# Hash attention with a feed-forward block: k and q read once and transposed on TensorE for the first batch, weights staged in pieces, feed-forward issued over the whole next batch

## The chip, the cores and the metric

One core of a Trainium2 chip. The metric is the device time of one execution in microseconds (us). "Profile" means the record of one profiled execution, "span" its length (about 2 us less than the time on the clock of the runs). The program runs on one core, so there is no second die to compare; runs more than 1.5% above the fastest of the same kernel are set aside as slow.

Engines: PE is TensorE, PEld its weight loads, DVE VectorE, ACT ScalarE, POOL GpSimd, SP the engine that issues most DMAs (SPq is its queue of instructions).

## The reference, cut to what matters

```python
# q, k, v: (4 batches, 8 heads, 768 tokens, 64); proj: (64, 6)
q_bucket = sum((q @ proj > 0) * 2**arange(6));  k_bucket likewise
scores = where(q_bucket == k_bucket, q @ k.T / 8, -1e9)
attn   = softmax(scores) @ v                    # per head
x      = attn as (4, 768, 512)                  # heads side by side
xn     = (x - mean) / sqrt(var + 1e-6) * g_ln
out    = x + max(xn @ w_ch1, 0) @ w_ch2         # 512 -> 2048 -> 512
```

The last line needs all heads of a batch, so a batch has two stages: attention, then feed-forward.

## The kernel before

The mask is folded into the score matmul: each row of q and k gets six extra columns (its hash bits as plus or minus one half, on the q side times a large number), so a score matmul contracts 64 + 6 = 70 rows. A "unit" is four heads; there are 8 units, two per batch. Attention is a chain of 192 steps (24 per unit). A step is one `scores` (two matmuls, one exp of 128x768 on ACT) and one `attend` of two steps earlier (six small matmuls). Preparation of the next unit, normalization, stores and feed-forward are put into the steps by a table, `at(step, function, ...)`, and each engine is given its share in that order.

Preparing a unit reads k and q twice, in two layouts: "hash" rows for the bits, "score" rows for the operand. The padded operand is then transposed by DMA:

```python
load_hash(...)                                   # hashnat: for the bits
load_rows(...)                                   # scorenat: for the operand
pad[:, :, 0:64] = cast(scorenat)                 # POOL
hashT = 32x32 transposes of hashnat              # DVE
hp    = projT.T @ hashT                          # PE, f32, four column groups side by side
pad[:, :, 64:70] = (transposed hp > 0) - 0.5     # DVE
opT   = DMA transpose of pad                     # SP queue
```

The feed-forward of a batch is a generator that yields after each of its 224 matmuls. This is the loop that drives it, cut (`...`):

```python
LAG, FF_DELAY, N_FF, BATCH, TAIL_MM = 2, 7, 224, 48, 45
# first[b] = b*48 + 1 + 48 + 7:  56, 104, 152, 200;   n_steps = 192
for b in range(B):
    z = b * BATCH + LAG - 1
    ...
    at(z + BATCH, rstd, b)                 # statistics, four Newton rounds: DVE
    at(z + BATCH, normalize, b, 0)         # DVE
    at(z + BATCH + 1, turn_x, b, 0)        # DMA transpose: xT
    at(z + BATCH + 1, normalize, b, 1)
    at(z + BATCH + 3, turn_x, b, 1)
while ...:
    scores(i); attend(i - LAG); run_step(i)
    if first[b] == i: ffq.append(feed_forward(b))
    if i < n_steps:
        target = 0.0
        for b in range(B):
            left = TAIL_MM if b == B - 2 else 0
            span = BATCH if b < B - 2 else n_steps - first[b]
            target += (N_FF - left) * min(max((i + 1 - first[b]) / span, 0.0), 1.0)
    else:
        target = done + 7
    while ffq and done < target:
        next(ffq[0]); done += 1
    i += 1
```

The f32 weights (8.4 MB) come in 1 MB pieces through two buffers (`hbuf`), from before step 0 to about step 43, and are cast by DVE.

The softmax here doesn't subtract the row's maximum and nothing guards it: scores larger than these inputs give would overflow.

Of the kernel before, what the change touches and what calls it, by code (L numbers as in the profile page):

```python
# [9 lines left out]

F32 = mybir.dt.float32
BF16 = mybir.dt.bfloat16
I32 = mybir.dt.int32
AOP = mybir.AluOpType
# [4 lines left out]
def kernel(  # L19
# [11 lines left out]
    nc = tc.nc  # L31
    P = 128

    B, H, S, D = q.shape
    NB = proj.shape[1]
    DM = moe_g_ln.shape[0]
    HID = moe_w_ch1.shape[1]
    assert DM == H * D and D == 64 and S == 768

    NS = S // P  # L40
    UH = 4
    NU = H // UH
    SL = UH * NS
    KB = D + NB
    VA = D + 1
    ND = DM // P
    NH = HID // P
    HALF = NS // 2
    QH = HALF * P

    scale = 1.0 / math.sqrt(D)
    BIG = 200.0
# [3 lines left out]
    consts = ctx.enter_context(tc.tile_pool(name="consts", bufs=1))  # L56
    prep = ctx.enter_context(tc.tile_pool(name="prep", bufs=1))
    work = ctx.enter_context(tc.tile_pool(name="work", bufs=1))
    ps_sc = ctx.enter_context(tc.tile_pool(name="ps_sc", bufs=2, space=bass.MemoryType.PSUM))
    ps_av = ctx.enter_context(tc.tile_pool(name="ps_av", bufs=2, space=bass.MemoryType.PSUM))  # L60
    ps_mm = ctx.enter_context(tc.tile_pool(name="ps_mm", bufs=2, space=bass.MemoryType.PSUM))
# [6 lines left out]
    proj_v = proj.rearrange("(j p) n -> p j n", p=32)  # L68
    for h in range(UH):
        nc.gpsimd.dma_start(  # L70
            out=projT[h * 32 : (h + 1) * 32, :, h * NB : (h + 1) * NB], in_=proj_v
        )
    bias_sb = consts.tile([P, 1], F32)
    nc.vector.memset(bias_sb, exp_bias)
    delta_m = consts.tile([P, P], BF16)
# [8 lines left out]
    g_sb = consts.tile([P, ND], F32)  # L84
# [8 lines left out]
    def at(i, fn, *args):  # L93
        todo.setdefault(i, deque()).append((fn, args))
# [7 lines left out]
    unit = {}  # L102
# [11 lines left out]
    def load_rows(ap, n, key, eng):  # L114
        b, u = divmod(n, NU)
        sn = prep.tile([P, UH, NS * D], F32, tag="scorenat", bufs=3, name="scorenat")
        eng.dma_start(
            out=sn,
            in_=ap[b, u * UH : (u + 1) * UH].rearrange("h (p s) d -> p h (s d)", s=NS),
        )  # L120
        loaded[(n, key, "rows")] = sn

    def pad_of(n, key):
        return pads[(2 * n + (key == "q")) % 3]

    def cast_rows(n, key):
        sn = loaded.pop((n, key, "rows"))
        nc.gpsimd.tensor_copy(  # L128
            pad_of(n, key)[:, :, 0:D], sn.rearrange("p h (s d) -> p (h s) d", d=D)
        )  # L130

    def hash_turn(n, key):
        hn = loaded.pop((n, key, "hash"))
        hT = prep.tile([P, 4, NS, 2, 32], F32, tag="hashT", bufs=1, name="hashT")
        for i in range(2):
            nc.vector.transpose(  # L136
                hT[:, 2 * i : 2 * i + 2].rearrange("p c s j t -> p (c s j t)"),
                hn[:, 2 * i : 2 * i + 2].rearrange("p c n -> p (c n)"),
            )
        half_done[(n, key)] = hT  # L140

    def hash_mm(n, key):
        hT = half_done.pop((n, key))
        hp = ps_mm.tile([P, 512], F32, tag="mm", name="hp")
        for j in range(2):
            for c in range(4):
                nc.tensor.matmul(  # L147
                    hp[c * 32 : (c + 1) * 32, 0 : NS * 32],
                    projT[:, j, :],
                    hT[:, c, :, j, :],  # L150
                    start=(j == 0), stop=(j == 1),
                )
        bits = prep.tile([P, NS, 32], F32, tag="bits", bufs=2, name="bits")
        nc.vector.transpose(bits.rearrange("p s n -> p (s n)"), hp[:, 0 : NS * 32])
        dst = pad_of(n, key).rearrange("p (h s) n -> p h s n", s=NS)[:, :, :, D:KB]
        src = bits[:, :, 0 : UH * NB].rearrange("p s (h n) -> p h s n", n=NB)
        nc.vector.tensor_scalar(
            dst, src, scalar1=0.0, scalar2=0.5, op0=AOP.is_gt, op1=AOP.subtract
        )
        if key == "q":  # L160
            nc.vector.tensor_scalar_mul(dst, dst, 4.0 * BIG)

    def turn(n, key, parts=1):
        tT = prep.tile([P, SL, P], BF16, tag="opT", bufs=4, name="opT")
        w = SL // parts
        for i in range(parts):
            nc.sync.dma_start_transpose(  # L167
                out=tT[:, i * w : (i + 1) * w, :],
                in_=pad_of(n, key)[:, i * w : (i + 1) * w, :].rearrange("p a n -> p (a n)"),
            )  # L170
        unit[(n, key)] = tT

    def value_cast(n):
# [18 lines left out]
    def plan_unit(n):  # L192

        z = (n - 1) * UNIT
        at(z + 0, cast_rows, n, "k")
        at(z + 0, hash_turn, n, "k")
        at(z + 3, hash_mm, n, "k")
        at(z + 5, turn, n, "k")
        at(z + 6, cast_rows, n, "q")
        at(z + 6, hash_turn, n, "q")  # L200
        at(z + 9, hash_mm, n, "q")
        at(z + 9, value_cast, n)
        at(z + 11, turn, n, "q")
        at(z + 15, value_sum, n)
        if n + 1 < B * NU:
            at(z + 3, load_hash, k, n + 1, "k", nc.sync)
            at(z + 3, load_rows, k, n + 1, "k", nc.sync)
            at(z + 9, load_hash, q, n + 1, "q", nc.sync)
            at(z + 9, load_rows, q, n + 1, "q", nc.sync)
            at(z + 15, load_rows, v, n + 1, "v", nc.sync)  # L210


    staged = {}

    def load_w1(o):
        st = work.tile([P, HID], F32, tag="hbuf", bufs=2, name="w1st")
        nc.sync.dma_start(out=st, in_=w1ap[:, o, :])
        staged[o] = st

    def fold_w1(o):  # L220
        nc.vector.tensor_scalar_mul(w1_sb[:, o, :], staged.pop(o), g_sb[:, o : o + 1])  # L221

    def load_w2(o):
        st = work.tile([P, 4, DM], F32, tag="hbuf", bufs=2, name="w2st")
        nc.sync.dma_start(out=st, in_=w2ap[:, o * 4 : (o + 1) * 4, :])
        staged[o] = st

    def cast_w2(o):
        nc.vector.tensor_copy(w2_sb[:, o * 4 : (o + 1) * 4, :], staged.pop(o))


    xs = {}
# [108 lines left out]
    def scores(i):  # L341
        b, u, h, t = steps[i]
        n = b * NU + u
        qT, kT = unit[(n, "q")], unit[(n, "k")]
        sc = ps_sc.tile([P, 2, 512], F32, tag="sc", name="sc")
        for f in range(2):
            nc.tensor.matmul(  # L347
                sc[:, f, 0:QH],
                kT[0:KB, h * NS + t, :],
                qT[0:KB, h * NS + f * HALF : h * NS + (f + 1) * HALF, :],  # L350
            )
        e = work.tile([P, 2, QH], BF16, tag="expb", bufs=4, name="expb")
        nc.scalar.activation(e, sc[:, :, 0:QH], AF.Exp, scale=scale, bias=bias_sb)  # L353
        exps[i] = e

# [31 lines left out]

    load_hash(k, 0, "k", nc.sync)
    load_hash(q, 0, "q", nc.scalar)
    load_rows(k, 0, "k", nc.sync)  # L390
    load_rows(q, 0, "q", nc.scalar)
    load_rows(v, 0, "v", nc.sync)
    for key in ("k", "q"):
        cast_rows(0, key)
        hash_turn(0, key)
        hash_mm(0, key)
        if key == "k":
            load_hash(k, 1, "k", nc.sync)
        turn(0, key, UH)
    value_cast(0)  # L400
    load_rows(k, 1, "k", nc.sync)
    load_hash(q, 1, "q", nc.sync)
    load_rows(q, 1, "q", nc.sync)
    value_sum(0)
    nc.sync.dma_start(out=g_sb, in_=moe_g_ln.rearrange("(o p) -> p o", p=P))
    load_w1(0)
    load_w1(1)
    load_rows(v, 1, "v", nc.sync)

    for n in range(1, B * NU):  # L410
        plan_unit(n)
    for o in range(4):
        at(8 + 5 * o, fold_w1, o)
        at(28 + 5 * o, cast_w2, o)
        if o < 2:
            at(8 + 5 * o, load_w1, o + 2)
            at(28 + 5 * o, load_w2, o + 2)
        else:
            at(8 + 5 * o, load_w2, o - 2)
    first = {}  # L420
    for b in range(B):
        z = b * BATCH + LAG - 1
# [15 lines left out]
    i = 0  # L438
    while i < n_steps + LAG + FF_DELAY + 1 or ffq or any(j >= i for j in todo):
        now[0] = i  # L440
        if i < n_steps:
            scores(i)
        if LAG <= i < n_steps + LAG:
            attend(i - LAG)
        run_step(i)
        for b in range(B):
            if first[b] == i:
                ffq.append(feed_forward(b))
        if i < n_steps:
            target = 0.0  # L450
            for b in range(B):
                left = TAIL_MM if b == B - 2 else 0
                span = BATCH if b < B - 2 else n_steps - first[b]
                target += (N_FF - left) * min(max((i + 1 - first[b]) / span, 0.0), 1.0)
# [3 lines that stand above are left out]
            try:  # L458
                next(ffq[0])
                done += 1  # L460
            except StopIteration:
                ffq.popleft()
        i += 1
# [30 lines left out]
```

## Time and profile before

| | before |
|---|---|
| time, median of 4 runs | 456.92 us (456.63 to 458.27) |
| span of the profile (of an execution of 459.3 us, slower than the four) | 457.5 us |
| PE busy / weight loads busy | 76% / 42% |
| DVE, ACT busy | 44%, 42% |

The first view is the page's table of 40 slices of 11.4 us. A digit is the busy share in tenths, PEclk the clock granted to PE, DMA the mean busy share of the 16 DMA engines. Ahead of the first clock record (30.2 us in this profile) the views print full clock, and that is no measurement: a hash took 2.35 us at 11.4 us, as long as at 75.4 us, where half clock is recorded, and 0.86 us at recorded full clock.

```profile
PE   0476247936499998856899998864999988449996
ACT  1065144844230329966112169952303199503020
PEclk9998555785799999996699999977999999759999
DMA  8999999995493017990961068965110130030101
```

Three regimes can be read. In slices 1 to 9 (to about 103 us) DMA is full while PE and ACT are half busy and PE's clock falls to half. From slice 11 on, ACT's row swings between 9 and 0: that is attention (ACT full, PE with gaps) alternating with feed-forward (PE full, ACT nearly idle). The last five slices are the tail: feed-forward of the last batch alone.

The alternation is plainer in the exps alone. This view gives the exp instruction (line 353) in six stretches: stretch and its length, busy time of ACT (number of exps that ran in it, whole or in part), granted clock, DMA share, GB/s. The DMA share can go above 1, since the whole time of a packet is counted in the stretch in which it starts.

```profile
60.00:72.00 12.00, 3.89 (x5) 0.50 1.12 268
144.00:156.00 12.00, 0.00 (x0) 1.00 0.12 44
168.00:180.00 12.00, 10.96 (x14) 1.00 0.63 154
240.00:252.00 12.00, 0.00 (x0) 1.00 0.12 45
276.00:288.00 12.00, 11.09 (x15) 1.00 0.86 197
336.00:348.00 12.00, 0.00 (x0) 1.00 0.13 49
```

Fifteen exps per 12 us is 0.79 us per step, ACT's limit; none at all runs during a feed-forward. At 60 us it is five.

Three waits of the first batch, the PE work of one step, and the wait before the last feed-forward, from the timeline: start, duration, engine, line, instruction, output and inputs, shapes, count, and in brackets how long the engine had been idle and what ended that.

```profile
54.07 0.38 PE L187 MATMUL vp<-vs,delta_m 128*128 128x260 bf16 x1 [9.66 <-POOL vs L181]
69.85 0.80 PE L347 MATMUL sc<-opT 70*128 70x384 bf16 x2 [7.64 <-DMA opT<-pad_85]
106.03 0.80 PE L347 MATMUL sc<-opT 70*128 70x384 bf16 x2 [10.13 <-DMA opT<-pad_87]
...
84.97 0.50 PE L347 MATMUL sc<-opT 70*128 70x384 bf16 x2
85.31 0.35 PE L364 MATMUL av<-vaug_92,expb 128*128 128x65 bf16 x6
85.49 0.49 PE L347 MATMUL sc<-opT 70*128 70x384 bf16 x2
...
406.98 1.44 PE L305 MATMUL h_4108<-xT,w_sb 128*128 128x384 bf16 x4 [11.65 <-DMA xT<-xn]
```

The first three are idle times of 8 to 10 us, at bottom waits for loads (vs is made from v, which had landed late) and for DMA transposes. Lines four to six show what a step costs PE when ACT does not hold it up: the next pair of score matmuls starts 0.52 us after the previous one. The Trainium skill, "TensorE: Matmul & The Clock Gate" (Step-by-step: what each phase is for), says that weight loads are pulled ahead of running matmuls; this trace agrees, since the six weight loads of `attend` take 0.38 us but matmuls and loads together take 0.52 us, less than the 0.32 us of the score matmuls plus 0.38 us.

### The profile page before, as it was taken

What the parts mean: (1) busy time and instruction counts of PE and PEld (TensorE: products, weight loads), DVE (VectorE), ACT (ScalarE), POOL (GpSimd) and SP (SyncE); (2) the same over time, 40 slices, a digit from 0 to 9 for tenths busy, and PEclk for the clock granted to TensorE, in tenths of its full rate; (3) what the DMA queues carried; (4) which work ended last, traced back from release to release, by engine and by line L of the source; (5) the groups of instructions that cost most, each with busy time, mean ns of one, the idle gap of its engine ahead of it and who ended that gap; (6) DMA issues with size and microseconds to landing.
All of it is one profiled execution on the core that took longest, in us unless ns stands there. A gap on an engine that the chain in (4) does not pass through costs nothing.

```text
span 457.5 us, 6762 instructions
## 1 busy us (share of the span) xinstructions
PE 345.7 (76%) x2688; PEld 190.4 (42%) x2696; DVE 202.7 (44%) x471; ACT 190.2 (42%) x257; POOL 71.0 (16%) x70
## 2 busy tenths in 40 slices
PE   0476247936499998856899998864999988449996
PEld 0143124524254545533445455532545455215452
DVE  1525125829832325949523227568323234642221
ACT  1065144844230329966112169952303199503020
POOL 5611513214011002314110004140000000000000
PEclk9998555785799999996699999977999999759999
DMA  8999999995493017990961068965110130030101
GB/s 200 282 202 352 193 277 356 249 291 128 111 243 129 1 69 177 223 225 6 249 182 47 23 123 210 225 114 110 28 71 0 70 71 1 1 69 1 69 1 69
DMA packets 91120, 62.32 MB, mean 136 GB/s; under 512 B 64976, under 2 KB 85456, under 8 KB 90576
## 3 DMA queue, kind: packets, MB, share of 16 engines
q1 hardware_dynamic: 89856, 60.31, 54.2%
q10 hardware_dynamic: 1104, 1.57, 1.3%
q8 instruction: 21, 0.34, 0.3%
q14 instruction: 11, 0.09, 0.1%
q0 software_dynamic: 128, 0.01, 0.0%
HBM read 39.85 MB, written 6.29 MB: 101 GB/s over the span
## 4 chain that ended last, share of the span: by engine, by line
PE 46%; DMA 21%; ACT 14%; DVE 9%; issue 4%; SPq 3%; POOL 1%; ACTq 0%; DVEq 0%
ACT expb L353 14%; DMA scorenat<-in_q_dram 4%; PE sc L347 3%; DMA scorenat<-in_k_dram 3%; DMA xT<-xn 3%; DMA opT<-pad_86 2%; DMA w1st<-in_moe_w_ch_dram 2%; DMA opT<-pad_85 2%; DMA opT<-pad_87 2%; PE hp L147 2%; SPq L167 2%; PE av L364 1%; DVE xn L275 1%; DMA hashnat<-in_q_dram 1%; DVE t L261 1%
## 5 line engine op out<-in xcount | busy, mean ns | idle before, releaser
L353 ACT ACTIVATE expb<-sc,bias_sb 128x768 bf16<-128x768 f32 x192 | 157.5, 921 | 106.4 <-PE sc L347 104.5
L347 PE MATMUL sc<-opT 70*128 70x384 bf16 x384 | 106.0, 361 | 45.4 <-DMA opT<-pad_85 11.4
L305 PEld LDWEIGHTS <-w_sb 128*128 128x128 bf16 x512 | 52.5, 103 | 78.2 <-issue 51.3
L364 PEld LDWEIGHTS <-expb 128*128 128x128 bf16 x1152 | 67.6, 105 | 33.4 <-issue 12.2
L347 PEld LDWEIGHTS <-opT 70*128 70x128 bf16 x384 | 35.2, 103 | 80.0 <-issue 79.2
L320 PEld LDWEIGHTS <-hbuf 128*128 128x128 bf16 x384 | 37.6, 98 | 45.7 <-issue 1.8
L376 DVE TENSOR_TENSOR nd<-av,vd 128x390 f32<-128x390 f32 x32 | 17.7, 554 | 45.0 <-PE av L364 45.0
L147 PE MATMUL hp<-hashT,projT 128*32 128x192 f32 x256 | 22.6, 436 | 17.9 <-DVE hashT L136 17.8
L136 DVE STREAM_TRANSPOSE hashT<-hashnat 128x768 f32<-128x768 f32 x32 | 29.2, 951 | 14.7 <-DMA hashnat<-in_k_dram 9.3
L364 PE MATMUL av<-vaug_91,expb 128*128 128x65 bf16 x432 | 28.1, 206 | 0.0
L364 PE MATMUL av<-vaug_92,expb 128*128 128x65 bf16 x432 | 27.5, 203 | 0.6 <-ACT expb L353 0.4
L382 DVE TENSOR_TENSOR x<-nd,rec 128x384 f32<-128x384 f32 x32 | 20.6, 643 | 1.1
L147 PEld LDWEIGHTS hp<-hashT,projT 128*32 128x32 f32 x256 | 8.9, 135 | 25.0 <-DVE hashT L136 21.5
L364 PE MATMUL av<-vaug_93,expb 128*128 128x65 bf16 x288 | 17.4, 198 | 0.0
L128 POOL CAST pad_85<-scorenat 128x1536 bf16<-128x1536 f32 x6 | 8.8, 1467 | 50.9 <-DMA scorenat<-in_k_dram 27.2
L238 DVE BATCH_NORM_STATS2 stats<-x 128x6 f32<-128x256 f32 (+1 forms) x48 | 16.1, 379 | 0.2
L179 POOL TENSOR_TENSOR scorenat<-scorenat 128x768 f32<-128x768 f32 x8 | 15.2, 1895 | 0.2
L128 POOL CAST pad_87<-scorenat 128x1536 bf16<-128x1536 f32 x5 | 7.3, 1467 | 50.4 <-DMA scorenat<-in_k_dram 30.4
L221 DVE TENSOR_SCALAR w_sb<-w1st,g_sb 128x2048 bf16<-128x2048 f32 x4 | 5.1, 1284 | 18.8 <-DMA w1st<-in_moe_w_ch_dram 18.8
L187 PE MATMUL vp<-vs,delta_m 128*128 128x260 bf16 x8 | 2.4, 299 | 13.3 <-POOL vs L181 13.3
L176 POOL CAST vaug_92<-scorenat 128x1536 bf16<-128x1536 f32 x3 | 4.4, 1472 | 51.3 <-DMA scorenat<-in_v_dram 51.3
L176 POOL CAST vaug_91<-scorenat 128x1536 bf16<-128x1536 f32 x3 | 4.7, 1582 | 45.6 <-DMA scorenat<-in_v_dram 45.5
(345 smaller groups left out, 383.5 us busy)
## 6 DMA issues: line engine op xcount, KB each, us to landing
hashnat<-in_k_dram SPq DMA_DIRECT2D x32, 192.0 KB, 4.9
scorenat<-in_k_dram SPq DMA_DIRECT2D x8, 768.0 KB, 7.4
scorenat<-in_v_dram SPq DMA_DIRECT2D x8, 768.0 KB, 5.6
out_dram<-x SPq DMA_DIRECT2D x24, 256.0 KB, 2.0
hashnat<-in_q_dram SPq DMA_DIRECT2D x28, 192.0 KB, 4.4
scorenat<-in_q_dram SPq DMA_DIRECT2D x7, 768.0 KB, 7.1
w1st<-in_moe_w_ch_dram SPq DMA_DIRECT2D x4, 1024.0 KB, 8.7
w2st<-in_moe_w_ch_dram SPq DMA_DIRECT2D x4, 1024.0 KB, 9.0
```

The costliest lines, as they stand in the source:

```text
L128: nc.gpsimd.tensor_copy(pad_of(n, key)[:, :, 0:D], sn.rearrange("p h (s d) -> p (h s) d", d=D))
L136: nc.vector.transpose(hT[:, 2 * i : 2 * i + 2].rearrange("p c s j t -> p (c s j t)"), hn[:, 2 * i : 2 * i + 2].rearrange("p c n -> p (c n)"),)
L147: nc.tensor.matmul(hp[c * 32 : (c + 1) * 32, 0 : NS * 32], projT[:, j, :], hT[:, c, :, j, :], start=(j == 0), stop=(j == 1),)
L179: nc.gpsimd.tensor_add(vn[:, :, 0:3, :], vn[:, :, 0:3, :], vn[:, :, 3:6, :])
L238: nc.vector.bn_stats(norm[b][:, s, part, :], xs[b][:, s, c0:c1])
L305: nc.tensor.matmul(hp[:, 0:QH], w1_sb[:, o, n * P : (n + 1) * P], xT[:, :, o, :], start=(o == 0), stop=(o == ND - 1),)
L320: nc.tensor.matmul(o2, hb[:, n, i * P : (i + 1) * P], w2_sb[:, n, :], start=(n == 0), stop=(n == NH - 1),)
L347: nc.tensor.matmul(sc[:, f, 0:QH], kT[0:KB, h * NS + t, :], qT[0:KB, h * NS + f * HALF : h * NS + (f + 1) * HALF, :],)
L353: nc.scalar.activation(e, sc[:, :, 0:QH], AF.Exp, scale=scale, bias=bias_sb)
L364: nc.tensor.matmul(av[:, s * VA : (s + 1) * VA], e[:, s // HALF, (s % HALF) * P : (s % HALF + 1) * P], va[:, h, t, :], start=(t == 0 and s ...
L376: nc.vector.tensor_add(nd, av[:, 0 : NS * VA].rearrange("p (s n) -> p s n", n=VA), vd[:, h : h + 1, :].to_broadcast([P, NS, VA]),)
L382: nc.vector.tensor_mul(xs[b][:, :, hd * D : (hd + 1) * D], nd[:, :, 0:D], rec.to_broadcast([P, NS, D]),)
```

## The change

Three things (smaller edits go with them: the loads of unit 2 are issued seven to ten steps later, `v` of the later units three steps earlier, and `expb` has three buffers instead of four):

1. Units 0 and 1 (the first batch) read k and q once, in hash layout. The operand comes from the same tile, and is transposed by PE (24 transposes per operand, copied out of PSUM by DVE or ACT) instead of by DMA. The hash bits then have to come out in another layout, for which the matmul uses a block-diagonal projection over the whole array and no longer four column groups side by side.
2. Weights are staged in 0.5 MB pieces: six in `hbuf` before step 0, six in the buffers of `x` that batch 1 and 2 will use, four in `hbuf` again.
3. The feed-forward target no longer counts the last batch. For it, `span` is 192 - 200 = -8, and `(i + 1 - 200) / -8` is at least 1 for every i below 192. So the target held 224 extra matmuls from the start, and every feed-forward was emitted whole in the step in which it began.

The diff, cut to its core:

```diff
+    projB = consts.tile([P, 2, P], F32)          # block-diagonal, one block per head
+    ident = consts.tile([P, P], BF16); make_identity(nc, ident)
...
+    def wide(n):
+        return n < NU                              # units 0 and 1
+    def cast_wide(n, key):                         # POOL: operand from the hash rows
+    def hash_mm_wide(n, key):
+        for f in range(2):
+            hp = ps_mm.tile([P, 512], F32, tag="mm", name="hpw")
+            for j in range(2):
+                nc.tensor.matmul(hp[:, 0 : w * 32], projB[:, j, :],
+                    hT[:, 2 * f : 2 * f + 2, :, j, :], start=(j == 0), stop=(j == 1))
+            nc.vector.transpose(...)
+    def turn_wide(n, key, engines):
+        for c in range(4):
+            tp = ps_mm.tile([P, 1024], BF16, tag="mm", name="tp")
+            for s in range(NS):
+                nc.tensor.transpose(tp[0:KB, s * P : (s + 1) * P], pad[:, c * NS + s, 0:KB], ident)
+            # copy to opT by DVE, or by DVE and ACT in turn for unit 0
...
         if n + 1 < B * NU:
-            at(z + 3, load_hash, k, n + 1, "k", nc.sync)
+            lag = 10 if wide(n) else 0
+            at(z + lag + 3, load_hash, k, n + 1, "k", nc.sync)      # q alike; v at z + lag + 12
...
-    for o in range(4):
-        at(8 + 5 * o, fold_w1, o)
-        at(28 + 5 * o, cast_w2, o)
-        ...
+    at(12, load_weights, "x", 3, (6, 7, 8))
+    at(14, load_weights, "x", 3, (9, 10, 11))
+    at(21, load_weights, "hbuf", 2, (12, 13, 14))
+    at(23, load_weights, "hbuf", 2, (15,))
+    for w in range(6):
+        at(15 + w, cast_weights, w)
+    for w in range(6, 12):
+        at(30 + w, cast_weights, w)
+    for w in range(12, 16):
+        at(38 + w, cast_weights, w)
...
-        e = work.tile([P, 2, QH], BF16, tag="expb", bufs=4, name="expb")
+        e = work.tile([P, 2, QH], BF16, tag="expb", bufs=3, name="expb")
...
             target = 0.0
-            for b in range(B):
+            for b in range(B - 1):
```

More of the change, by code (lines that the diff above doesn't have):

```diff
@@ L9 @@
 from concourse._compat import with_exitstack
+from concourse.masks import make_identity
 F32 = mybir.dt.float32
@@ L72 @@
         )
+    projB = consts.tile([P, 2, P], F32)
+    nc.vector.memset(projB, 0.0)
+    for h in range(UH):
+        nc.gpsimd.dma_start(
+            out=projB[h * 32 : (h + 1) * 32, :, h * 32 : h * 32 + NB], in_=proj_v
+        )
+    ident = consts.tile([P, P], BF16)
+    make_identity(nc, ident)
     bias_sb = consts.tile([P, 1], F32)
@@ L130, in cast_rows @@
         )
+    def wide(n):
+        return n < NU
+    def cast_wide(n, key):
+        hn = loaded[(n, key, "hash")]
+        nc.gpsimd.tensor_copy(
+            pad_of(n, key)[:, :, 0:D], hn.rearrange("p c (s d) -> p (c s) d", d=D)
+        )
+    def hash_mm_wide(n, key):
+        hT = half_done.pop((n, key))
+        bits = work.tile([P, SL, 32], F32, tag="xn", bufs=2, name="bitsw")
+        w = SL // 2
+        for f in range(2):
+            hp = ps_mm.tile([P, 512], F32, tag="mm", name="hpw")
+            for j in range(2):
+                nc.tensor.matmul(
+                    hp[:, 0 : w * 32], projB[:, j, :], hT[:, 2 * f : 2 * f + 2, :, j, :],
+                    start=(j == 0), stop=(j == 1),
+                )
+            nc.vector.transpose(
+                bits[:, f * w : (f + 1) * w, :].rearrange("p a n -> p (a n)"), hp[:, 0 : w * 32]
+            )
+        dst = pad_of(n, key)[:, :, D:KB]
+        nc.vector.tensor_scalar(
+            dst, bits[:, :, 0:NB], scalar1=0.0, scalar2=0.5,
+            op0=AOP.is_gt, op1=AOP.subtract,
+        )
+        if key == "q":
+            nc.vector.tensor_scalar_mul(dst, dst, 4.0 * BIG)
     def hash_turn(n, key):
@@ L161, in hash_mm, with turn @@
             nc.vector.tensor_scalar_mul(dst, dst, 4.0 * BIG)
-    def turn(n, key, parts=1):
+    def turn_wide(n, key, engines):
         tT = prep.tile([P, SL, P], BF16, tag="opT", bufs=4, name="opT")
-        w = SL // parts
-        for i in range(parts):
-            nc.sync.dma_start_transpose(
-                out=tT[:, i * w : (i + 1) * w, :],
-                in_=pad_of(n, key)[:, i * w : (i + 1) * w, :].rearrange("p a n -> p (a n)"),
-            )
+        dst = tT.rearrange("p (h s) (c t) -> p c h s t", s=NS, c=4)
+        pad = pad_of(n, key)
+        for c in range(4):
+            tp = ps_mm.tile([P, 1024], BF16, tag="mm", name="tp")
+            for s in range(NS):
+                nc.tensor.transpose(
+                    tp[0:KB, s * P : (s + 1) * P], pad[:, c * NS + s, 0:KB], ident
+                )
+            src = tp[0:KB, 0 : NS * P].rearrange("p (s h t) -> p h s t", h=UH, t=32)
+            if engines[c % len(engines)] is nc.scalar:
+                nc.scalar.copy(dst[0:KB, c], src)
+            else:
+                nc.vector.tensor_copy(dst[0:KB, c], src)
+        unit[(n, key)] = tT
+    def turn(n, key):
+        tT = prep.tile([P, SL, P], BF16, tag="opT", bufs=4, name="opT")
+        nc.sync.dma_start_transpose(out=tT, in_=pad_of(n, key).rearrange("p a n -> p (a n)"))
         unit[(n, key)] = tT
@@ L194, in plan_unit @@
         z = (n - 1) * UNIT
-        at(z + 0, cast_rows, n, "k")
+        cast = cast_wide if wide(n) else cast_rows
+        mm = hash_mm_wide if wide(n) else hash_mm
+        at(z + 0, cast, n, "k")
         at(z + 0, hash_turn, n, "k")
-        at(z + 3, hash_mm, n, "k")
-        at(z + 5, turn, n, "k")
-        at(z + 6, cast_rows, n, "q")
+        at(z + 3, mm, n, "k")
+        if wide(n):
+            at(z + 5, turn_wide, n, "k", (nc.vector,))
+            at(z + 11, turn_wide, n, "q", (nc.vector,))
+        else:
+            at(z + 5, turn, n, "k")
+            at(z + 11, turn, n, "q")
@@ L200, in plan_unit @@
+        at(z + 6, cast, n, "q")
         at(z + 6, hash_turn, n, "q")
-        at(z + 9, hash_mm, n, "q")
+        at(z + 9, mm, n, "q")
         at(z + 9, value_cast, n)
-        at(z + 11, turn, n, "q")
         at(z + 15, value_sum, n)
         if n + 1 < B * NU:
-            at(z + 3, load_hash, k, n + 1, "k", nc.sync)
-            at(z + 3, load_rows, k, n + 1, "k", nc.sync)
-            at(z + 9, load_hash, q, n + 1, "q", nc.sync)
-            at(z + 9, load_rows, q, n + 1, "q", nc.sync)
-            at(z + 15, load_rows, v, n + 1, "v", nc.sync)
@@ L213 @@
-    staged = {}
-    def load_w1(o):
-        st = work.tile([P, HID], F32, tag="hbuf", bufs=2, name="w1st")
-        nc.sync.dma_start(out=st, in_=w1ap[:, o, :])
-        staged[o] = st
-    def fold_w1(o):
-        nc.vector.tensor_scalar_mul(w1_sb[:, o, :], staged.pop(o), g_sb[:, o : o + 1])
-    def load_w2(o):
-        st = work.tile([P, 4, DM], F32, tag="hbuf", bufs=2, name="w2st")
-        nc.sync.dma_start(out=st, in_=w2ap[:, o * 4 : (o + 1) * 4, :])
-        staged[o] = st
-    def cast_w2(o):
-        nc.vector.tensor_copy(w2_sb[:, o * 4 : (o + 1) * 4, :], staged.pop(o))
+            lag = 10 if wide(n) else 0
@@ new lines, in plan_unit, with load_weights @@
+            at(z + lag + 3, load_hash, k, n + 1, "k", nc.sync)
+            at(z + lag + 3, load_rows, k, n + 1, "k", nc.sync)
+            at(z + lag + 9, load_hash, q, n + 1, "q", nc.sync)
+            at(z + lag + 9, load_rows, q, n + 1, "q", nc.sync)
+            at(z + lag + 12, load_rows, v, n + 1, "v", nc.sync)
+    WP = 1024
+    N1 = ND * HID // WP
+    w1flat = w1_sb.rearrange("p o h -> p (o h)")
+    w2flat = w2_sb.rearrange("p o d -> p (o d)")
+    staged = {}
+    def load_weights(tag, bufs, pieces):
+        st = work.tile([P, 3, WP], F32, tag=tag, bufs=bufs, name="wst")
+        for i, w in enumerate(pieces):
+            if w < N1:
+                c = w * WP % HID
+                src = w1ap[:, w * WP // HID, c : c + WP]
+                dst = st[:, i, :]
+            else:
+                r = WP // DM
+                src = w2ap[:, (w - N1) * r : (w - N1 + 1) * r, :]
+                dst = st[:, i, :].rearrange("p (o d) -> p o d", d=DM)
+            nc.sync.dma_start(out=dst, in_=src)
+            staged[w] = st[:, i, :]
@@ L232, with cast_weights @@
+    def cast_weights(w):
+        st = staged.pop(w)
+        if w < N1:
+            o = w * WP // HID
+            nc.vector.tensor_scalar_mul(
+                w1flat[:, w * WP : (w + 1) * WP], st, g_sb[:, o : o + 1]
+            )
+        else:
+            nc.vector.tensor_copy(w2flat[:, (w - N1) * WP : (w - N1 + 1) * WP], st)
     xs = {}
@@ L389 @@
     load_hash(q, 0, "q", nc.scalar)
-    load_rows(k, 0, "k", nc.sync)
-    load_rows(q, 0, "q", nc.scalar)
-    load_rows(v, 0, "v", nc.sync)
     for key in ("k", "q"):
-        cast_rows(0, key)
+        cast_wide(0, key)
         hash_turn(0, key)
-        hash_mm(0, key)
         if key == "k":
             load_hash(k, 1, "k", nc.sync)
-        turn(0, key, UH)
+            load_rows(v, 0, "v", nc.sync)
+        hash_mm_wide(0, key)
+        turn_wide(0, key, (nc.vector, nc.scalar))
     value_cast(0)
-    load_rows(k, 1, "k", nc.sync)
     load_hash(q, 1, "q", nc.sync)
-    load_rows(q, 1, "q", nc.sync)
+    load_rows(v, 1, "v", nc.sync)
+    nc.sync.dma_start(out=g_sb, in_=moe_g_ln.rearrange("(o p) -> p o", p=P))
+    load_weights("hbuf", 2, (0, 1, 2))
+    load_weights("hbuf", 2, (3, 4, 5))
     value_sum(0)
-    nc.sync.dma_start(out=g_sb, in_=moe_g_ln.rearrange("(o p) -> p o", p=P))
-    load_w1(0)
-    load_w1(1)
-    load_rows(v, 1, "v", nc.sync)
     for n in range(1, B * NU):
         plan_unit(n)
-    for o in range(4):
-        at(8 + 5 * o, fold_w1, o)
-        at(28 + 5 * o, cast_w2, o)
-        if o < 2:
-            at(8 + 5 * o, load_w1, o + 2)
-            at(28 + 5 * o, load_w2, o + 2)
-        else:
-            at(8 + 5 * o, load_w2, o - 2)
+    at(12, load_weights, "x", 3, (6, 7, 8))
[8 more added lines that the diff above has]
+        at(38 + w, cast_weights, w)
     first = {}
```

## The prediction

> **What bounds it now.** The table of busy time by stretch shows three regimes. (1) 0 to about 117 us, first batch: DMA share near 1 in every 12 us stretch to 108 us (28.7 MB, about 266 GB/s). The score/exp stream stands still for DMA: the timeline has PE gaps of 10 us (waits for v), 8 and 10 us (waits for opT transposes). (2) 117 to 395 us, batches 1 to 3: attention and feed-forward take turns. For about 50 us per batch no exp runs (117-168, 215-266, 313-363); then exp runs every 0.79 us (ACT-bound) while PE idles between steps. The reason is in the loop: for the last batch the span is negative (192-200), so the target always contains 224 extra matmuls, and each feed-forward is emitted at once. One period is about 97 us. (3) 395 to 457.5 us, tail: 11.65 us wait for xT, a cold start (four groups at 1.28 us, not 0.65-0.81), 224 matmuls, last store.
>
> **What the change does, costed.**
> - Spreading. Where ACT does not stall it, two score-and-attend steps follow each other after 0.52 us (84.97 to 85.49, 189.48 to 190.00). Feed-forward of one batch costs 32 groups at 0.65 us plus 6 at 3.45 us, 41.5 us; the 0.81/0.65 alternation of the burst (two PSUM buffers) should go. Steps 56 to 192: 136 x 0.52 = 71 us, 2.8 feed-forwards = 116 us, nine hashes at 0.8 us = 7 us: 195 us, PE-bound. I add about 12 us: around steps 97-99 and 145-147 DVE is taken for some 12 us by hash transpose, statistics, the rsqrt chain and normalization, and PSUM buffers for feed-forward and hash wait behind it. Another 10 us for clock dips and small waits. The Trainium skill, "TensorE: Matmul & The Clock Gate" (The HAM clock gate), says the clock halves after an idle window of about 3.4 us; this trace agrees (granted clock 0.50 at 48-84 us, after gaps). So about 217 us, against 278 us now.
> - First batch. k and q of units 0 and 1 are read once: 3.1 MB less, four DMA transposes less. But weights and unit 2 loads move behind step 12, so DMA stays the limit for steps 30-48. Added on PE and DVE: per operand 24 PE transposes with four DVE/ACT copies of 70x768 (estimate 0.8 us each, from the 128x768 exp of 0.74 us), about 3 us; and hash matmuls that no longer use four column groups side by side: about 2.6 us warm, 4-5 us cold, instead of 0.8. Startup is serial: first exp at about 28 us, not 25.5. Step 56 at about 106 us instead of 117.
> - Tail: the 45 held-back matmuls (9 us) now really fill the wait for xT; no cold start: about 60 us instead of 62. expb with three buffers costs nothing.
>
> **Predicted:** 106 + 217 + 60 = 383 us; 8 in 10 between 365 and 404. Faster by over 2%: 0.96; within 2%: 0.03; slower: 0.01.
>
> **Signs.** Right if: exps are spaced 1.3-1.6 us through batches 1-3, with no 50 us hole in the ACT row; PE 90% or more and granted clock 1.0 there but for dips at batch boundaries; DMA transposes of opT fall from 22 to 12; first exp at or after 25.5 us; waits of scores on opT remain once, near step 48; PE not idle for 11 us after the last attend.
>
> **What would make it wrong.** Interleaving could cost PE more than the sum (weight loads no longer hidden, DVE evacuations late): then the period approaches 97 us. If the first batch is not DMA-bound after the change, step 56 comes near 90 us. If DVE stands in order on a weight cast whose load is late, everything behind it stops, and step 56 stays at 117 us.

## The result

| | before | after |
|---|---|---|
| median of 4 runs | 456.92 us | 390.14 us (386.11 to 391.62) |
| ratio | | 0.852, 95% interval 0.845 to 0.859 |
| span of the profile | 457.5 us | 384.2 us |

A ratio is the mean time of one kernel's fast runs over that of the other's fast runs of the same rounds, so it is not quite the ratio of the medians. The profiled execution of the changed kernel was its fastest (386.11 us); a second profile, taken with the experiments below, is of an execution of 391.05 us and is used where a few us matter.

Since every step has exactly one exp, counting exps gives the time at which a step begins. All step times in this document are read in this way, from the profiled executions:

| step begins (us) | before | after | after, second profile |
|---|---|---|---|
| 0 | 25.5 | 31.7 | 29.2 |
| 24 | 70.7 | 60.4 | 58.0 |
| 48 | 106.9 | 89.6 | 92.4 |
| 56 | 115.5 | 98.1 | 100.5 |
| 104 | 213.7 | 186.8 | 192.0 |
| 152 | 310.8 | 265.4 | 270.0 |
| 191 | 394.0 | 319.0 | 323.7 |
| end | 457.5 | 384.2 | 389.1 |

| stretch | before | after | after, second |
|---|---|---|---|
| to step 56 | 115.5 | 98.1 | 100.5 |
| steps 56 to 191 | 278.5 | 220.9 | 223.2 |
| step 191 to the end | 63.5 | 65.2 | 65.4 |

So 15 to 17 us came from the first batch, 55 to 58 us from the middle, where e1 shows that it is the spreading, and nothing from the tail. The same table of slices (9.6 us each) of the changed kernel:

```profile
PE   0678988827289999995999999959999999599995
ACT  1015589944348656762587568625876783031220
PEclk9966999975769999998999999998999999899999
DMA  8559999994399598703994999028401000510102
```

PE's row now reads 9 throughout from slice 13 on, with a single 5 where a batch ends; ACT's row has no run of zeros before the tail. The exps alone (now line 426), same columns as before:

```profile
60.00:72.00 12.00, 11.09 (x15) 1.00 1.07 300
84.00:96.00 12.00, 4.61 (x6) 0.55 0.62 173
144.00:156.00 12.00, 6.88 (x8) 1.00 0.95 241
168.00:180.00 12.00, 4.33 (x5) 1.00 0.15 39
240.00:252.00 12.00, 7.21 (x8) 1.00 0.06 23
276.00:288.00 12.00, 7.74 (x10) 1.00 0.01 1
```

Eight to ten exps per 12 us, without a pause: 1.2 to 1.5 us per step, set by PE. At a batch boundary (168 us) there are five. What PE does within such a step, from the timeline (start, duration, instruction, count):

```profile
190.03 0.49 PE L420 MATMUL sc<-opT 70*128 70x384 bf16 x2
190.36 0.35 PE L437 MATMUL av<-vaug_103,expb 128*128 128x65 bf16 x6
190.54 0.49 PE L378 MATMUL h_2345<-xT,w_sb 128*128 128x384 bf16 x2
190.87 0.49 PE L378 MATMUL h_2362<-xT,w_sb 128*128 128x384 bf16 x2
191.19 0.49 PE L420 MATMUL sc<-opT 70*128 70x384 bf16 x2
```

The attention part still takes 0.51 us (190.03 to 190.54), the four feed-forward matmuls 0.65 us. In such a step the mixing costs PE nothing.

The startup, the one remaining wait for a DMA transpose, and the first feed-forward, from the same view:

```profile
11.44 5.17 PE L159 MATMUL hpw<-hashT,projB 128*128 128x384 f32 x8 [11.44 <-DVE hashT L178]
20.98 5.46 PE L159 MATMUL hpw<-hashT,projB 128*128 128x384 f32 x8 [0.18 <-DVE hashT L178]
31.72 3.72 ACT L426 ACTIVATE expb<-sc,bias_sb 128x768 bf16<-128x768 f32 x4 [0.89 <-PE sc L420]
88.72 0.80 PE L420 MATMUL sc<-opT 70*128 70x384 bf16 x2 [8.55 <-DMA opT<-pad_98]
104.73 1.44 PE L378 MATMUL h_1225<-xT,w_sb 128*128 128x384 bf16 x4 [6.54 <-DMA xT<-xn]
```

And a batch boundary, and the held-back matmuls in the tail:

```profile
176.39 2.82 DVE L348 TENSOR_SCALAR xn<-x,mv,y 128x512 bf16<-128x512 f32 x6
179.13 0.37 DVE L196 STREAM_TRANSPOSE bits<-hp 128x192 f32<-128x192 f32 x1
179.56 0.59 PE L393 MATMUL o_2218<-w_sb,hbuf 128*128 128x512 bf16 x2 [4.18 <-DVE bits L196]
...
330.73 5.04 PE L393 MATMUL o_4214<-w_sb,hbuf 128*128 128x512 bf16 x15 [4.17 <-DVE x L399]
```

DVE works from 169 to 179 us without a break on the last head, the statistics, the Newton rounds and the normalization of the batch that just ended. The evacuations of PSUM that PE needs come behind that in DVE's program: the matmuls of the hash ended at 173.3 us, their evacuation (second line) began at 179.1 us, after the normalization. PE stops for 4.2 us, in the tail once more.

### The profile page after: what moved, and what is told of

The parts are those of the page before. It is cut to its first block, busy times and chain, and to the rows that moved or that the text cites. A ratio compares the mean times of both kernels' runs of the same rounds, so it can differ in the third digit from the quotient of the medians.

```text
span 384.2 us, 6912 instructions
## 1 busy us (share of the span) xinstructions
PE 323.8 (84%) x2741; PEld 187.5 (49%) x2760; DVE 205.6 (54%) x496; ACT 198.5 (52%) x261; POOL 72.1 (19%) x76
## 4 chain that ended last, share of the span: by engine, by line
PE 58%; DVE 20%; DMA 15%; issue 2%; ACT 2%; SPq 1%; POOL 1%; DVEq 0%; ACTq 0%
PE sc L420 11%; PE av L437 6%; DMA hashnat<-in_k_dram 5%; DVE x L455 3%; DMA scorenat<-in_v_dram 3%; DMA hashnat<-in_q_dram 3%; DVE xn L348 2%; DVE nd L449 2%; DMA wst<-in_moe_w_ch_dram 2%; DMA opT<-pad_98 2%; DVE x L399 2%; PE hp L189 2%; ACT expb L426 2%; PE hpw L159 1%; PE o_4214 L393 1%
## 5 line engine op out<-in xcount | busy, mean ns | idle before, releaser
L426 ACT ACTIVATE expb<-sc,bias_sb 128x768 bf16<-128x768 f32 x192 | 168.4, 905 | 97.2 <-PE sc L420 95.7
L420 PE MATMUL sc<-opT 70*128 70x384 bf16 x384 | 97.9, 338 | 15.1 <-DMA opT<-pad_98 8.6
L437 PEld LDWEIGHTS <-expb 128*128 128x128 bf16 x1152 | 62.5, 99 | 28.0 <-issue 3.7
L378 PEld LDWEIGHTS <-w_sb 128*128 128x128 bf16 x512 | 45.1, 98 | 36.9 <-issue 15.4
L420 PEld LDWEIGHTS <-opT 70*128 70x128 bf16 x384 | 37.3, 100 | 49.0 <-issue 26.4
L178 DVE STREAM_TRANSPOSE hashT<-hashnat 128x768 f32<-128x768 f32 x32 | 29.2, 950 | 9.0 <-DMA hashnat<-in_k_dram 9.0
L159 PE MATMUL hpw<-hashT,projB 128*128 128x384 f32 x32 | 17.3, 706 | 11.6 <-DVE hashT L178 11.6
L437 PE MATMUL av<-vaug_103,expb 128*128 128x65 bf16 x432 | 25.5, 196 | 0.0
L437 PE MATMUL av<-vaug_102,expb 128*128 128x65 bf16 x432 | 25.5, 196 | 0.0
L437 PE MATMUL av<-vaug_104,expb 128*128 128x65 bf16 x288 | 17.2, 197 | 0.0
L159 PEld LDWEIGHTS hpw<-hashT,projB 128*128 128x128 f32 x32 | 8.5, 278 | 17.6 <-DVE hashT L178 11.4
L137 POOL CAST pad_98<-scorenat 128x1536 bf16<-128x1536 f32 x4 | 5.9, 1467 | 46.1 <-DMA scorenat<-in_k_dram 25.1
L137 POOL CAST pad_96<-scorenat 128x1536 bf16<-128x1536 f32 x4 | 5.9, 1467 | 45.5 <-DMA scorenat<-in_k_dram 24.9
L137 POOL CAST pad_97<-scorenat 128x1536 bf16<-128x1536 f32 x4 | 5.9, 1467 | 40.7 <-DMA scorenat<-in_k_dram 21.0
L189 PE MATMUL hp<-hashT,projT 128*32 128x192 f32 x192 | 11.6, 365 | 1.4 <-DVE hbuf L387 1.4
L163 DVE STREAM_TRANSPOSE bitsw<-hpw 128x384 f32<-128x384 f32 x8 | 4.7, 583 | 14.6 <-PE hpw L159 14.6
## 6 DMA issues: line engine op xcount, KB each, us to landing
hashnat<-in_k_dram SPq DMA_DIRECT2D x32, 192.0 KB, 4.4
hashnat<-in_q_dram SPq DMA_DIRECT2D x28, 192.0 KB, 4.7
hashnat<-in_q_dram ACTq DMA_DIRECT2D x4, 192.0 KB, 6.2
```

Source lines behind the costliest of these rows:

```text
L137: nc.gpsimd.tensor_copy(pad_of(n, key)[:, :, 0:D], sn.rearrange("p h (s d) -> p (h s) d", d=D))
L159: nc.tensor.matmul(hp[:, 0 : w * 32], projB[:, j, :], hT[:, 2 * f : 2 * f + 2, :, j, :], start=(j == 0), stop=(j == 1),)
L178: nc.vector.transpose(hT[:, 2 * i : 2 * i + 2].rearrange("p c s j t -> p (c s j t)"), hn[:, 2 * i : 2 * i + 2].rearrange("p c n -> p (c n)"),)
L189: nc.tensor.matmul(hp[c * 32 : (c + 1) * 32, 0 : NS * 32], projT[:, j, :], hT[:, c, :, j, :], start=(j == 0), stop=(j == 1),)
L378: nc.tensor.matmul(hp[:, 0:QH], w1_sb[:, o, n * P : (n + 1) * P], xT[:, :, o, :], start=(o == 0), stop=(o == ND - 1),)
L420: nc.tensor.matmul(sc[:, f, 0:QH], kT[0:KB, h * NS + t, :], qT[0:KB, h * NS + f * HALF : h * NS + (f + 1) * HALF, :],)
```

## The experiments

All gave correct results. Each set ran on one chip with its own runs of the kernel before, whose median was 457.1 to 458.1 us. Ratios are against those. e1 to e4 are one set, after_again, e5, e6 and e8 another, e9 and e10 a third; a difference between runs of two sets is less sure than one within a set.

| run | edit | median us | ratio (95%) |
|---|---|---|---|
| after_again | the changed kernel | 390.93 | 0.853 (0.850 to 0.857) |
| e1 | before + spreading alone | 403.53 | 0.880 (0.876 to 0.884) |
| e2 | after without the spreading | 445.68 | 0.972 (0.967 to 0.976) |
| e3 | after, boundary work split | 386.68 | 0.844 (0.839 to 0.849) |
| e4 | after, weights staged as before | 394.67 | 0.861 (0.856 to 0.865) |
| e5 | after, loads first | 383.89 | 0.840 (0.837 to 0.844) |
| e6 | after, k and q read twice | 399.67 | 0.873 (0.870 to 0.876) |
| e8 | e3, feed-forward later | 382.13 | 0.833 (0.829 to 0.837) |
| e9 | after, unit 0 as before | 394.69 | 0.865 (0.858 to 0.872) |
| e10 | e5 + e8, weight casts earlier | 374.02 | 0.818 (0.813 to 0.823) |

| step begins (us) | e1 | e2 | e3 | e4 | e5 | e6 | e8 | e9 | e10 |
|---|---|---|---|---|---|---|---|---|---|
| 0 | 25.7 | 30.7 | 29.0 | 29.7 | 31.0 | 28.5 | 29.4 | 25.7 | 29.9 |
| 48 | 106.2 | 95.4 | 91.5 | 101.6 | 85.0 | 98.8 | 90.4 | 95.6 | 88.5 |
| 56 | 115.0 | 104.7 | 100.1 | 110.9 | 93.2 | 107.2 | 99.2 | 103.8 | 96.9 |
| 100 | 190.6 | 197.8 | 179.5 | 185.4 | 171.6 | 187.4 | 174.3 | 182.9 | 171.4 |
| 104 | 203.7 | 201.0 | 185.5 | 197.3 | 184.4 | 199.3 | 180.7 | 194.8 | 177.9 |
| 120 | 226.6 | 266.7 | 213.0 | 220.1 | 207.2 | 222.3 | 208.0 | 217.6 | 205.7 |
| 191 | 336.2 | 380.6 | 318.3 | 329.3 | 316.7 | 331.9 | 314.1 | 327.2 | 312.6 |
| end | 401.3 | 444.8 | 384.5 | 394.6 | 382.0 | 398.3 | 377.6 | 392.5 | 376.1 |

### The comparison run

> The changed kernel itself, for a comparison on one chip. 388 to 392 us.

390.93 us: the changed kernel repeats on another chip.

### e1: the spreading alone

```diff
 # the kernel before
-            for b in range(B):
+            for b in range(B - 1):
```

> The kernel before with one edit: the feed-forward target no longer counts the last batch, so that the feed-forward is spread. Theory (the spreading is worth 55 us between steps 56 and 191, the rest of the change about 17 us before step 56): step 56 stays at 115 us, steps 56 to 191 take about 221 us, tail 65 us, time 400 to 408 us. Rival (spreading only works with the faster first batch and the fewer DMA transposes; each part alone gives little): over 425 us.

403.53 us. Step 56 at 115.0 us, steps 56 to 191 in 221.2 us, tail 65.1 us: the theory in all three stretches. One token is worth 54 us; neither the faster first batch nor the fewer DMA transposes are needed for it.

### e2: everything but the spreading

```diff
 # the changed kernel
-            for b in range(B - 1):
+            for b in range(B):
```

> The changed kernel with only the spreading undone (target counts the last batch again). Theory: step 56 at 98 us, then 278 us as before, tail 63 us: 436 to 444 us. Rival: under 420 us, if most of the gain came from the first batch.

445.68 us, just above the range. The middle and the tail were as expected (275.9 and 64.2 us); step 56 came at 104.7 instead of 98 us. The expectation had been taken from the fastest profile of the changed kernel; the first batch differs by several us from execution to execution (98.1, 100.5, 104.7 and, in e3, which differs only from step 49 on, 100.1; step 48 at 89.6, 92.4, 95.4 and 91.5 us). These four profiles are what the first batches of the other runs are compared with. The two parts add up: 0.880 times 0.972 is 0.855, the whole change 0.852 to 0.853.

### e3: the work at a batch boundary split

```diff
-        at(z + BATCH, normalize, b, 0)
-        at(z + BATCH + 1, turn_x, b, 0)
-        at(z + BATCH + 1, normalize, b, 1)
-        at(z + BATCH + 3, turn_x, b, 1)
+        at(z + BATCH + 1, newton, b, 2, False)    # two of the four rounds
+        at(z + BATCH + 2, newton, b, 2, True)
+        at(z + BATCH + 3, normalize, b, 0)
+        at(z + BATCH + 4, turn_x, b, 0)
+        at(z + BATCH + 4, normalize, b, 1)
+        at(z + BATCH + 6, turn_x, b, 1)
```

> The changed kernel with the DVE work at a batch boundary (statistics, four Newton rounds, normalization, some 9 us in one piece) split over five steps, so that evacuations of feed-forward PSUM come in between. Theory: the stretches of steps 100 to 104 and 148 to 152, 12 us each where four ordinary steps take 5.8 us, shrink to 6 or 7 us, and the wait of held-back matmuls in the tail (4.2 us) goes: 12 to 16 us less, about 376 us. Rival (the hole is made by loads or DMA transposes for the next unit): unchanged within 3 us of the changed kernel.

386.68 us: only 4 us less, not 12 to 16, and the 4 are little more than the noise (0.844 against 0.852 and 0.853, in different sets). The local part of the theory held: steps 100 to 104 took 6.0 us (11.9 and 12.0 in the two profiles of the changed kernel), steps 148 to 152 also 6.0 (12.0 and 11.9). But steps 104 to 120 took 27.5 us instead of 22.8 to 23.0. The timeline of e3 shows what PE waits for there, in the same columns as above:

```profile
185.19 0.34 PE L442 MATMUL av<-vaug,expb 128*128 128x65 bf16 x6
188.62 1.58 PE L383 MATMUL h<-xT,w_sb 128*128 128x384 bf16 x5 [3.08 <-DMA xT<-xn]
```

The next feed-forward now begins before its input is there. From the last `attend` of the batch (at 175.2 us) to the arrival of xT the chain took 13 us. In the changed kernel the stop for the evacuation had covered it: its feed-forward began at 186.7 us, 16 us after its last `attend` (170.5 us), with xT already there. A wait had been taken away, and it came back at the next one. In total over the profile, PE waited 12.5 us behind DVE at two boundaries and in the tail in the changed kernel (three stops of 4.2 us) and 6.5 us for xT; in e3 these three stops are gone, and four waits for xT make 19.9 us (first line the changed kernel, second e3; who waited for whom, us in total, times, longest):

```profile
PE h_1225 L378 <- DMA xT<-xn: 6.5, 1, 6.5
PE h L383 <- DMA xT<-xn: 19.9, 4, 10.5
```

### e8: the split, and a later feed-forward

```diff
 # e3
-    FF_DELAY = 7
+    FF_DELAY = 10
-    TAIL_MM = 45
+    TAIL_MM = 64
```

> The changed kernel with the boundary work split as in e3, and with the feed-forward starting three steps later (10 for 7) and 64 for 45 matmuls held back for the tail. Theory (in e3 the wait moved: matrix multiplication of the next feed-forward now stood still for xT, whose chain from the last attend takes 13 us, or 9 steps): neither the evacuations nor xT are waited for, steps 56 to 191 take 205 to 210 us and the tail stays at 65 us: 374 to 379 us. Rival (PE is at its limit, whatever is not waited for here is waited for elsewhere): within 3 us of e3.

382.13 us; one of the four runs, 385.25, counts as slow, and the fast three have the median 382.03, 8.9 less than the changed kernel on the same chip. That is less than e3 too (0.833 against 0.844, intervals apart), though above the expected range: steps 56 to 191 took 214.9 us, not 205 to 210, and the tail 63.5. The wait for xT is gone, at every boundary and in the tail: a feed-forward follows the last one without a gap. By stretch, the gain over e3 is not where the theory looked first: steps 100 to 120 took 33.7 us (e3 33.5, the changed kernel 34.7 and 35.0) and steps 148 to 168 30.7 us in both; it lies in steps 56 to 64 (3.0 us, with about 14 feed-forward matmuls fewer in them) and in the tail (2.7 us, though with about 14 more, because PE is idle 5.2 us in it and no longer 8.5). The delay and the 64 were not tried apart. Two holes remain. At the end of the first batch DVE works through the boundary chain and, in the same steps 50 to 53, four weight casts, and PE waits for a hash transpose behind them (first line). And at later boundaries a hash matmul waits for an evacuation that stands behind the second half of the normalization, two hash transposes and the last additions of a head (second line), after which PE was granted half clock for 3.4 us; steps 104 to 120 took 27.3 us, 27.5 in e3:

```profile
108.51 2.35 PE L189 MATMUL hp<-hashT,projT 128*32 128x192 f32 x16 [8.46 <-DVE hashT L178]
...
184.59 0.86 PE L189 MATMUL hp<-hashT,projT 128*32 128x192 f32 x16 [2.18 <-DVE x L404]
```

### e5: loads first

```diff
     load_hash(k, 0, "k", nc.sync)
     load_hash(q, 0, "q", nc.scalar)
+    load_rows(v, 0, "v", nc.sync)
+    nc.sync.dma_start(out=g_sb, ...)
+    load_weights("hbuf", 2, (0, 1, 2))
+    load_weights("hbuf", 2, (3, 4, 5))
     for key in ("k", "q"):
         ...    # load_hash(k, 1) waits here for a free hashnat buffer
     ...        # the same four lines removed below
```

> The changed kernel with v of unit 0, g and the first six weight pieces issued right after k of unit 0, ahead of the loads that wait for a free hashnat buffer. Theory (the first batch ends when DMA has moved what stands before the transposes of unit 2, and DMA was only 60 per cent busy in the first 24 us): 3.1 MB are moved earlier, step 48 comes 6 to 9 us earlier, time 381 to 385 us. Rival (the first batch is limited by the serial start and by DVE): first exp and step 48 unchanged or later, 389 us or more.

383.89 us, step 48 at 85.0 us, earlier than in all four profiles with the order of the changed kernel (89.6 to 95.4). The stretches of the changed kernel (first two lines) and of e5 (last two) show the idle DMA time that was used. Columns: stretch, busy us (instructions) of PE, weight loads, DVE, ACT, POOL, granted clock, DMA share, GB/s.

```profile
0.00:12.00 12.00, 0.56 (x1) 0.50 (x2) 2.17 (x6) 1.28 (x1) 10.81 (x22) 1.00 0.65 132
12.00:24.00 12.00, 9.76 (x37) 5.55 (x36) 4.53 (x9) 1.59 (x2) 4.60 (x4) 0.82 0.58 160
```

```profile
0.00:12.00 12.00, 0.00 (x0) 0.00 (x0) 1.95 (x6) 1.28 (x1) 10.78 (x21) 1.00 0.90 197
12.00:24.00 12.00, 9.60 (x36) 5.36 (x37) 4.67 (x8) 1.59 (x2) 6.21 (x7) 0.88 1.02 335
```

In the changed kernel the SP queue stood still behind `load_hash(k, 1)`, which waits for a buffer, and everything after it, although ready to go, stood too: the first weight piece was issued at 24.6 us, in e5 at 6.6 us. The first exp came no earlier (31.0 us), and still step 48 did.

### e6: k and q read a second time, for nothing

```diff
     load_rows(v, 1, "v", nc.sync)
+    for n in range(2):
+        load_rows(k, n, "unused", nc.sync)
+        load_rows(q, n, "unused", nc.sync)
```

> The changed kernel that reads k and q of units 0 and 1 a second time, as before, but uses the second copy for nothing: 3.1 MB more. Theory (DMA-bound first batch): step 48 about 10 us later, 398 to 402 us. Rival (the reads fill idle DMA time; the gain in the first batch came from the DMA transposes that went): within 3 us of the changed kernel.

399.67 us, 8.7 more than the changed kernel on the same chip. The extra 3.1 MB at the 300 GB/s that DMA moved at 48 to 72 us are 10 us. Step 48 came at 98.8 us, later than in all four profiles. With e5 this shows that DMA bounds the first batch of the changed kernel once its first 24 us, in which the DMA engines are busy 62% to 66%, are past.

### e4: the old staging of weights

```diff
-    load_weights("hbuf", 2, (0, 1, 2)); load_weights("hbuf", 2, (3, 4, 5))
+    load_w1(0); load_w1(1)
     # and the steps at which pieces are loaded and cast, as in the kernel before
```

> The changed kernel with the weights staged as before (1 MB pieces, two hbuf buffers, from step 8 on). Theory (the first batch is bound by DMA bytes, not by where weights are staged): within 5 us of the changed kernel. Rival (staging in early free buffers is what lets the first batch end early): step 56 later by 10 us or more, 400 us or more.

394.67 us: 0.861 against 0.852 and 0.853, so the new staging is worth about 4 us, at the edge of the noise (the intervals overlap). By the total the theory held. Step 56 came at 110.9 us in its profile, though, 6 to 13 us later than in the profiles of the changed kernel's order, so that the rival's sign was there in part: where pieces wait for a buffer, the transfers behind them in the queue wait too (the third piece waited 11.6 us, and k of unit 2, behind it, was issued at 46.1 us, 33.9 in the changed kernel). Part was made up in steps 56 to 64: 20.4 us, 22.5 and 24.2 in the changed kernel.

### e9: unit 0 prepared as before

```diff
-        return n < NU
+        return 0 < n < NU        # and unit 0 through load_rows, hash_mm, turn in four parts
```

> The changed kernel with unit 0 prepared as in the kernel before (rows read a second time, four column groups for its hash matmuls, DMA transposes in four parts), unit 1 as changed. Theory (the later first exp comes from the serial hash matmuls of 5.2 us each at half clock and the PE transposes with their copies): first exp back at about 25.5 us instead of 29 to 31.7; but 1.6 MB more are read and two DMA transposes more run in a batch that is bound by DMA, so the time is within 4 us of the changed kernel. Rival (an early first exp is worth its full 4 to 6 us): 385 to 387 us.

394.69 us. The first exp returned to 25.7 us, so the new preparation costs the start 3.5 to 6 us; but step 48 came at 95.6 us, no earlier than with it (89.6 to 95.4). The rival, 385 to 387 us, is out: the earlier start did not help a batch that waits for DMA, though e9 also moves more bytes, so it does not price the start alone. The expected 4 us held by the medians (3.8), not by the ratios, which are 0.865 and 0.853 (5.6 us); e9 ran in another set than after_again.

### e10: a version that beats both

```diff
 # e5 and e8 together, and
-        at(38 + w, cast_weights, w)      # w = 12 .. 15: steps 50 to 53
+        at(30 + w, cast_weights, w)      # steps 42 to 45
```

> Loads first (e5), boundary work split, later feed-forward and 64 matmuls held back (e8), and the last four weight casts eight steps earlier (steps 42 to 45 instead of 50 to 53). If the two gains add up (7 us and 9 us, in different stretches): 373 to 377 us. If one ends in the other's wait: 379 us or more.

374.02 us, 0.818 of the kernel before and, dividing the ratios, 0.958 of the changed kernel. The gains of e5 and e8 over the changed kernel (7.0 and 8.9 us) make 15.9 us; 16.9 us came, with the earlier casts in it (e10 ran in the set of e9, so this compares two sets). Its profiled run was its slowest (377.88 us). Its rows of the slice table:

```profile
PE   0568888826399999999799999898999999999995
PEclk9998999975869999999899999999999999999999
```

## Why the prediction was right

It said 383 us, 365 to 404; the median is 390.1. The mechanism was right, and three of its terms were off in size, in part against each other. In its own stretches (106, then 217 to the end of the last `attend`, then 60 us) the two profiles have 98.1, 223.7 and 62.4 us, and 100.5, 226.0 and 62.7 us. That the first of them sums to 384.2 us, so close to 383, is luck.

- **Spreading: right.** 217 us were predicted for steps 56 to 191; 220.9 and 223.2 were measured, 221.2 with the spreading alone (e1). The two sources of the estimate could be read from the trace of before: the step of 0.52 us where ACT did not stall PE, and the feed-forward's 0.65 and 3.45 us per group. In steps 64 to 96 a step took 1.48 and 1.51 us in the two profiles; 0.52 plus 41.5/48 makes 1.39, to which the prediction added hashes and waits apart. This is also what the Trainium skill advises, "Perfetto Trace Analysis" (Optimization Strategy): where the most contended engine changes over time, "performance may be improved by interleaving those regimes". The trace agrees: before, a batch took 97 us (steps 104 to 152), after, 78 to 79 us, and PE's busy share rose from 76% to 84%.
- **DVE at batch boundaries: right in cause and size, and in place within a few steps** ("I add about 12 us", steps 97 to 99 and 145 to 147). Steps 100 to 104 and 148 to 152 each took 6 us more than with the split chain of e3. What the prediction did not see is that this wait hid another, for xT; removing the first alone gained only 4 us.
- **First batch: the term was too pessimistic.** Step 56 was predicted at 106 us instead of 117; 98.1 and 100.5 were measured, and 104.7 in e2, instead of 115.5. That DMA stays the limit was right (e5, e6), and the startup was right in kind: the hash matmuls of an operand took 5.2 and 5.5 us in unit 0 and 2.8 us at full clock (4 to 5 cold and 2.6 warm predicted), an operand's transposes and copies 3.1 us (27.8 to 30.8 us). The first exp was later still, 29.2 to 31.7 us instead of 28. What was mis-sized is "3.1 MB less, four DMA transposes less": the predicted 11 us are about what the 3.1 MB of reads make at 266 GB/s (11.8 us), so the transposes seem to have got no time of their own. They move bytes too: the page totals below fall by 6.3 MB, of which 3.1 MB are reads of HBM, so the other 3.1 MB are the four transposes. Up to step 48 DMA moved 28.4 MB before (266 GB/s) and 22.2 MB after (248 and 240 GB/s). The 6.2 MB are 23 us at 266 GB/s, an estimate; 17.3 and 14.5 us came (e2: 11.5). The slower first 24 us (146 and 154 GB/s, 238 before) cost about 8 us of them, an estimate too. No run reads once and transposes by DMA, so what the transposes are worth in time is not isolated; e6 gives 8.7 us for the reads.
- **Tail: the step "about 60 us instead of 62" failed.** From the end of the last `attend` it was 62.2 us before (395.3 to 457.5) and 62.4 us after (321.8 to 384.2). The held-back matmuls fill the wait and the last feed-forward needs no cold start (44.5 us from its first matmul to the start of the last addition, 46.8 before), but the third group of the held-back matmuls needs a PSUM buffer whose evacuation lies behind the statistics, the Newton rounds and the first half of the normalization (4.2 us), and then runs partly at half clock; the last feed-forward began 13.8 us after the last `attend`, not 11.7. In e3, where the chain is split, the 38 matmuls left after the last `attend` ran in one go in 8.4 us, and PE then waited 4.3 us for xT.
- **Signs.** opT transposes by DMA fell from 22 to 12, one wait of scores for opT is left, near step 48, exps are spaced 1.2 to 1.5 us, the granted clock is 1.0 but for single dips at boundaries: all as said.

The page totals on which the first-batch term rests, before (two lines) and after (two lines):

```profile
DMA packets 91120, 62.32 MB, mean 136 GB/s; under 512 B 64976, under 2 KB 85456, under 8 KB 90576
HBM read 39.85 MB, written 6.29 MB: 101 GB/s over the span
DMA packets 77168, 56.03 MB, mean 146 GB/s; under 512 B 52560, under 2 KB 70992, under 8 KB 77136
HBM read 36.71 MB, written 6.29 MB: 112 GB/s over the span
```

**Still open.** The hole at the first feed-forward (steps 56 to 64 take 20 us in e10, where eight steps at 1.45 us would be 12) was not taken apart further. Why the first batch differs by up to 7 us between executions of the same instruction order was not tried. Nor was the buffer count of `expb` tried by itself; no wait for it shows.

## What to carry to other kernels

Look for stages that alternate on two engines: the profile shows it as one engine's row swinging between 9 and 0 while the other's swings against it, and a scheduler that is meant to interleave them should be checked for emitting everything at once. When a wait is removed, ask which dependency is ready next and when: in e3 most of the gain came back as a wait for xT, and in e8, where that was moved too, part of it came back as a wait for the next unit's hash. When a transfer is counted, count on-chip DMA transposes as bytes too. And in a stage bound by DMA, issue what is ready before what waits for a buffer on the same queue.

## What the Trainium skill lacked or had wrong

- "TensorE: Matmul & The Clock Gate" (PE-mode transpose) gives about 275 ns for a transpose in one kernel's context, and no time from one start to the next. Here a transpose of 128x70 took 219 ns and, at full clock, one started every 56 ns (twelve in 0.83 us): for a throughput estimate the duration is four times too long. The page also says that the full clock does not engage for transposes, and no run here speaks against that: in unit 0 the full clock was granted at 16.2 and 26.4 us, at the end of the hash matmuls, and was gone again at 19.6 and 29.9 us, after stretches in which PE did nothing but transposes.
- No page has a measured time of a small f32 matmul, with or without column groups; the passes of an f32 matmul and the gain of column groups are stated, but apart from each other. Here the hash of one operand took 0.86 us with four column groups and 2.83 us with block-diagonal matmuls over the whole array, both at full clock, 3.3 times as long.
- "DMA: Bandwidth & Descriptors" (Issuing engines are not separate DMA queues) says that issuing from several engines only saves issue time. It does not spell out that a queue whose head waits for a buffer holds back all that follows: putting 3.1 MB of weights and 0.8 MB of v ahead of such a load took 7 us off (e5; issuing them from another engine was not tried).
